# One PSUM tile per bank, 32-bit words in the weight conversion, and a new written order in a fused mLSTM and FFN kernel

## The chip, the core and the metric

The kernel runs on one core of a Trainium2 chip. The metric is the device time of one execution in microseconds (us), as the median of several runs. The engines go by their short names in the profile: PE is TensorE's matmul side and PEld its weight load, DVE is VectorE, ACT is ScalarE, POOL is GpSimd and SP issues the DMAs.

## What is computed

```python
for t in range(S):                    # q,k,v: (4 batches, 8 heads, 768 steps, 40)
    m_new = np.maximum(f_gate[:, :, t] + m, i_gate[:, :, t])
    f_stab, i_stab = np.exp(f_gate[:, :, t] + m - m_new), np.exp(i_gate[:, :, t] - m_new)
    m = m_new
    C = f_stab * C + i_stab * einsum(v_t, k_t);  n = f_stab * n + i_stab * k_t
    y[:, :, t] = sigmoid(o_gate) * (C q_t) / maximum(abs(n . q_t), 1)
x = y as (3072 tokens, 320)
h = x @ w_in                          # (320, 2048)
g = where(h > 0, h, exp(minimum(h, 0)) - 1)
out = g @ w_out                       # (2048, 320)
```

The two weight matrices arrive as 64-bit floats. The matmuls of the FFN take each operand as a high and a low part, and multiply three of the four pairs of parts.

## The kernel before

The tokens are 24 tiles of 128 (n = 0 to 23), six chunks of time for each of four batches. For each tile the attention does, in this order: `kq` and `us` (matmuls into the PSUM tile `pa`), a scan `ws`, products and state updates on DVE or POOL, `y` (matmuls into `pb`), a division, `turn` (three transposes through `pb`), and `xh`, `xl`, the two parts of the FFN's input. Two tiles make a block (kb = 0 to 11), 256 tokens wide.

For each block the FFN runs through 16 slices f of 128 columns of the inner width. One step of it is `L1` (eight matmuls into one bank of the PSUM tile `ph`, banks taken in turns, L659), `relu` (ACT, reads `ph`, L666), `exp` (ACT, in place, L668), `elu` (DVE, reads `ph` again, L670), `gh` (the high part, on ACT, DVE or POOL, L219), `gl` (the low part, on DVE or POOL, L675) and `L2` (six matmuls that add into `pc`, one bank for each of the block's two tiles, L682). There are 12 x 16 = 192 such steps. After a block's last slice, `os` copies `pc` out.

The weights of a group of four slices must be converted first. There are 18 conversions, of 512 or 640 columns: a load of 64-bit words into `wide`, then on the high halves `abs` (L311 or L313), `clip` (L317), `shift` (L321), on the low halves `frac` (ACT, L324), on the high halves `sign` (ACT, L329), then `join` (POOL, L338), `hi` (L345 or L347) and `lo` (DVE, L351). So that matmuls have work while weights are still coming, SPLITS lets some blocks run through part of the width first; the sums of such a part are stored to DRAM and loaded again (`sumstore`, `sumload`).

The first SPREAD_BY_PE tiles get their gate factors by small matmuls (`spread`, `spreadb`, into `ph` or `pc`), all others by DMAs that read them back from DRAM (`wdload`, `bbload`).

PLACES gives each operation its place in one order of the whole program and, by a letter, its engine where there is a choice. Each engine and SP's queue work through their own operations in that order. The semaphores between engines are put in by the framework, from what each instruction reads and writes in which tile. The keys in the calls of `op` only assert that PLACES is a legal order.

Of the kernel before, what the change touches and what calls it, by code (L numbers as in the profile page):

```python
# [19 lines left out]
P = 128  # L20

HI_MIN = 2.0**-14
# [4 lines left out]
    3g 27 6 17 15v 10g 8g 49g 21g 0g 4g 2 26v 35 37 24 30 42 50 58 29 61v 62 63 55 59 68 74 79 36 33 67 75 77 70  # L27
    78 81 85 100 90 104 51 101 109 112 106 110 117 138 144 73 120 147 149 123 127 153 164 168 113 155 173 181 176
    192 210 237 262 154 203 218 230 207 226 240 270 277 175 266 274 279 252 256 284 298 341 219 288 296 308 275
    309 315 326 400 253 350 364 369 321 334 373 383 391 302 404 412 417 397 418 424 451 459 328 325 394v 434 440  # L30
    374 389 444 477 500 507g 512 382 465 471 476 421 435 489 508 516 436 518 523 530 487 520 535 545 552 453 522v
    528 549 492 537 558 575v 590 498 559 564 572 531 565 578 586 595 544 596 605 610 616 624 630 639v 644 566 604
    613 625 642 646 650 659 662 1 9 11 13 12 16 19 14 22 31 53 111 108 18 23a 20 25 7 57v 44 34 52 48 54 56 60 66
    69 65 71 72 76 83 86 89g 91 94 97a 103 115 121 38 41 45 87v 129 64 46 80 93g 82 107 96 116 119 122 125 124 136
    139 140 142 143 145a 146 152 156 5 28 32 39 40 99 47 43 114 135 137 160 162 158 190a 161 170 174 178 180 185
    217 169 184 187 193 196 205 250 182 198 231 238 249 258 261 208 216 236 241 245 260 265 291v 307 272 338 98 95
    92 84 88 131 128 133v 199 126 130 132 151 179 159 172 177 188 194 202 204 206g 209 211 213a 215 220 224 134
    118 141 105 102 157 165 195v 223 163 189g 200 201 225g 212 214 221v 228 232 243 246 247 251 254 257v 259 263
# [12 lines left out]
    708 747 678 684 693 697 699 710 752 705 711 715 723 731 744 767 706 718 721 724 727 748g 773 732 749 750 753
    755 762 776 714 782 786 775 803 831 741 756 760 766 768v 771g 810 761 769 772 778 784g 788g 830 781 789 791
    799 802 807 836 787 794 797 801 818g 824g 862 804 812 814 819 828 835 870 817 847 851 852 853g 854g 890 840
    845 849 866 871g 882g 893 855 864 867 872 891v 894g 898 701 905 952 809 925 1042 569 468 330 509 244 547 335
    675v 734 670 677 636 683 696g 691 682 689 692 698 717 730 738 740g 742 746 751v 757 765 770 614 606 592 293
    619 461 457 720v 737 704 713 712 726 754 785 716v 733 736v 790 798 805v 808 811g 813 816 820a 827 833 837 881
    886 888 892 899 904g 930 884 897 900 903 915v 918g 948 902 910 911 914 916 920g 954 907 921 922 923 927g 949g
    974 924 932 933 939 942v 967 980 935 955 958 962 965 970g 992 960 971 973 977 984 987g 999 968 976 978 983
    986g 989 1003 985 990 991 994 996v 1001 1015 988 995 997 1002 1004g 1007 1020 1000 1005 1006 1009 1010v 1012g
    1024 1008 1013 1014 1016 1018v 1023 1033 1011 1017 1019 1022 1025g 1028g 1047 1027 1030 1031 1034 1038v 1041g  # L60
    1052 1029 1035 1036 1040 1048 1050g 1056 1037 1045 1046 1049 1051 1053 1061 1067v 1106 1073 1324 504 597 501
    603 722 709 780 792v 822 774 779g 793 796 841 826 815 823 838 839 850 856v 857 859 863 869 874a 877 889 895
    743 739 783 777 729 719 745 842v 901 795 800g 843 848 896g 909 832 878 885v 906 919 926 928 929 931 934 940
    944 950 953 439 725 728 758g 860 829 763 936 844 858g 861 951 846 943 947a 1043 1054 1055 1058 1060v 1076g
    1087 1065 1070 1075 1078 1086g 1088g 1109 1069 1080 1082 1092 1096 1115 1130 1094 1100 1104 1108 1114v 1117g
    1135 1099 1118 1120 1122 1136v 1140g 1157 1123 1131 1133 1141 1144 1153 1165 1145 1152 1155 1158 1162v 1163
    1180 1150 1159 1160 1164 1167v 1169g 1183 1161 1166 1168 1171 1172 1176g 1205 1170 1177 1178 1185 1192g 1193
    1215 1174 1181 1182 1191 1204 1208 1227 1194 1201 1203 1210 1214v 1219g 1232 1200 1212 1216 1233 1235g 1237
    1247 1223 1229 1231 1238 1241g 1246g 1251 1236 1243 1245 1248 1249g 1253g 1263 1240 1250 1252 1254 1256 1257
    1268 1274 1316 1288 1534 868 806 821 834 825 865 759 912 981 887 908g 913 917 1032g 957 945 961 964 982 1081  # L70
    1090 1091 1095 1097 1098 1103 1107 1110 1112 1044 880 883 966 873 956 876 1068 1021 998 1063 1077 1079 1105g
    1084 1066v 1083 1085 1101 1119 1125v 1126 1129g 1132 1134 1137a 1142 1147 1149 1255 1260 1262 1264 1266v 1269g
    1298 1258 1265 1267 1270 1271 1273 1317 1272 1277 1278 1280 1284g 1287 1322 1276 1281 1283 1289 1291g 1309
    1330 1293 1300 1310 1320 1323v 1326 1341 1304 1315 1318 1325 1328 1329g 1346 1327 1331 1332 1334 1335 1337
# [100 lines left out]
def tile_mlstm_then_elu_ffn(  # L175
# [29 lines left out]

# [12 lines left out]
    def copy(e, o, i):  # L218
        nc.scalar.copy(o, i) if e == "ACT" else eng[e].tensor_copy(o, i)  # L219
# [568 lines left out]
```

## Time and profile before

| | |
|---|---|
| runs | 573.17 us median of 3 (570.69 to 574.26) |
| the profiled execution | 575.71 us, of which 573.9 us from the first to the last instruction |
| mean granted TensorE clock | 0.985 of full speed |

The profiled execution is 2.5 us above the median and has 1.8 us outside its span. Every row below is from this one execution.

### The profile page before, as it was taken

The numbers are of one execution on the slowest core, as the hardware profiler recorded it, in microseconds if no ns is written. First come the engines' busy times: TensorE is split into PE (matmuls) and PEld (weight loads), VectorE is DVE, ScalarE is ACT, GpSimd is POOL, SyncE is SP. The second block draws the span as 40 slices with busy tenths as digits, with TensorE's granted clock in tenths as the row PEclk, the third lists the DMA queues.
The fourth block names the chain that finished last, engine by engine and source line by source line (L and its number), as shares of the span: only waits on it lengthen the run. The fifth ranks groups of instructions, "written<-read, shape, count | busy, mean of one in ns | idle before, by whom it ended". The sixth has DMA issues, their size and how long they took to land.

```text
span 573.9 us, 15807 instructions
## 1 busy us (share of the span) xinstructions
PE 478.8 (83%) x6574; PEld 441.1 (77%) x6574; DVE 315.8 (55%) x749; ACT 280.0 (49%) x650; POOL 161.7 (28%) x240
## 2 busy tenths in 40 slices
PE   5478887887889888998888889888888989889876
PEld 5467776876889878887777778778878979778765
DVE  6878777666777455654544447455355553334221
ACT  6858988986443344433333334432334434433333
POOL 4313313223244314423133112313211133132111
PEclk9999999899999899999999999998999999989899
DMA  7764454460344401510420322040321400000000
GB/s 218 246 203 161 140 176 132 143 211 17 98 146 115 118 1 30 152 54 28 129 76 2 97 51 64 5 123 2 97 74 44 123 0 3 24 1 1 23 2 23
DMA packets 21951, 48.13 MB, mean 84 GB/s; under 512 B 4184, under 2 KB 10008, under 8 KB 21880
## 3 DMA queue, kind: packets, MB, share of 16 engines
q1 hardware_dynamic: 21880, 47.13, 27.3%
q8 instruction: 51, 0.84, 0.6%
q14 instruction: 20, 0.16, 0.1%
HBM read 41.35 MB, written 5.77 MB: 82 GB/s over the span
## 4 chain that ended last, share of the span: by engine, by line
PE 56%; ACT 20%; DVE 13%; issue 6%; DMA 3%; SPq 1%; POOL 1%; ACTq 0%; POOLq 0%; DVEq 0%
PE ph L659 35%; PE pc L682 14%; DVE e L670 9%; ACT e L666 7%; ACT e L668 6%; PE pb L567 3%; ACT wide L324 2%; DMA f_d<-dec 2%; ACT wide L329 2%; PE pa L507 1%; PE pa L518 1%; ACT gh L219 1%; PE pb L625 1%; DVE w L489 1%; DVE gl L675 1%
## 5 line engine op out<-in xcount | busy, mean ns | idle before, releaser
L659 PE MATMUL ph<-xh,w 128*128 128x256 f32 x960 | 210.1, 300 | 64.4 <-DVE e L670 47.0
L659 PEld LDWEIGHTS ph<-xh,w 128*128 128x128 f32 x960 | 155.6, 194 | 88.8 <-DVE e L670 64.6
L670 DVE SCALAR_TENSOR_TENSOR e<-e,ph 128x256 f32<-128x256 f32 x192 | 80.1, 419 | 200.9 <-ACT e L668 95.9
L666 ACT ACTIVATE e<-ph 128x256 f32<-128x256 f32 x192 | 73.1, 384 | 213.9 <-PE ph L659 163.6
L682 PE MATMUL pc<-w,gh 128*128 128x320 f32 x768 | 176.8, 317 | 0.1
L682 PEld LDWEIGHTS pc<-w,gh 128*128 128x128 f32 x768 | 129.5, 194 | 1.8 <-DVE den L601 0.8
L659 PE MATMUL ph<-xl,w 128*128 128x256 f32 x576 | 126.3, 288 | 0.2 <-issue 0.2
L682 PE MATMUL pc<-w,gl 128*128 128x320 f32 x384 | 121.2, 316 | 1.0 <-DVE gl L675 0.7
L659 PEld LDWEIGHTS ph<-xl,w 128*128 128x128 f32 x576 | 98.0, 194 | 0.2 <-DVE xl L630 0.2
L675 POOL TENSOR_TENSOR gl<-e,gh 128x256 fp32r<-128x256 f32 x76 | 58.6, 772 | 116.8 <-ACT gh L219 55.7
L668 ACT ACTIVATE e<-e 128x256 f32<-128x256 f32 x192 | 79.4, 418 | 5.3
L682 PEld LDWEIGHTS pc<-w,gl 128*128 128x128 f32 x384 | 73.9, 192 | 2.5 <-DVE gl L675 1.6
L219 POOL CAST gh<-e 128x256 fp32r<-128x256 f32 x55 | 25.6, 466 | 136.1 <-DVE e L670 127.8
L675 DVE TENSOR_TENSOR gl<-e,gh 128x256 fp32r<-128x256 f32 x116 | 51.8, 453 | 19.2 <-ACT gh L219 10.7
L219 ACT CAST gh<-e 128x256 fp32r<-128x256 f32 x84 | 33.3, 404 | 30.7 <-DVE e L670 29.4
L338 POOL TENSOR_TENSOR narrow<-narrow,wide 128x512 int32<-128x512 int32 (+1 forms) x18 | 26.0, 1446 | 70.8 <-ACT wide L329 27.8
L489 DVE TENSOR_TENSOR_SCAN w<-w,ones 128x512 f32<-128x512 f32 x22 | 29.6, 1346 | 0.1
L329 ACT ACTIVATE wide<-wide,tiny 128x512 f16<-128x512 f32 (+1 forms) x18 | 28.4, 1578 | 0.3
L324 ACT ACTIVATE wide<-wide 128x512 int16<-128x512 uint32 (+1 forms) x18 | 26.4, 1483 | 2.6 <-DMA wide<-in_w_in 2.6
L567 PE MATMUL pb<-va,w 64*32 64x41 f32 x1536 | 22.0, 207 | 3.4 <-issue 3.3
L567 PE MATMUL pb<-C,qk 40*64 40x41 f32 x704 | 17.5, 233 | 6.1 <-DVE xl L630 3.8
L567 PEld LDWEIGHTS pb<-va,w 64*32 64x32 f32 x1536 | 18.4, 113 | 5.2 <-issue 3.9
(86 smaller groups left out, 420.3 us busy)
## 6 DMA issues: line engine op xcount, KB each, us to landing
vko<-in_vko SPq DMA_DIRECT2D x24, 480.0 KB
qk<-in_qk SPq DMA_DIRECT2D x48, 160.0 KB
w<-f_d SPq DMA_DIRECT2D x44, 128.0 KB
wide<-in_w_out SPq DMA_DIRECT2D x8, 640.0 KB
wide<-in_w_in SPq DMA_DIRECT2D x8, 512.0 KB
out<-os SPq DMA_DIRECT2D x24, 160.0 KB
bb<-b_d SPq DMA_DIRECT2D x44, 80.0 KB
sum<-os SPq DMA_DIRECT2D x10, 160.0 KB
```

Of the source, the lines that this page charges most:

```text
L219: nc.scalar.copy(o, i) if e == "ACT" else eng[e].tensor_copy(o, i)
L324: lambda e: nc.scalar.mul(quarters[:, :, 0], low.bitcast(U32), 2.0**-29),
L329: nc.scalar.activation(quarters[:, :, 1].bitcast(mybir.dt.float16), high.bitcast(F32), AF.Sign, bias=tiny)
L338: lambda e: nc.gpsimd.tensor_add(word, word, low),
L489: lambda e: nc.vector.tensor_tensor_scan(flat, src, ones.rearrange("p h t -> p (h t)"), 0.0, op0=ALU.mult, op1=ALU.add),
L567: nc.tensor.matmul(y[at, two, j, :], a, m, start=(at.start, two) not in begun, stop=False, skip_group_check=True)
L659: nc.tensor.matmul(h, a[g][:, fs], m, start=(i == 0), stop=(i == len(prods) - 1))
L666: lambda e, h=h, ev=ev: nc.scalar.activation(ev, h, AF.Relu, scale=-1.0), (KHP,), (KE,))
L668: lambda e, ev=ev: nc.scalar.activation(ev, ev, AF.Exp, scale=-1.0), (), (KE,))
L670: lambda e, h=h, ev=ev: nc.vector.scalar_tensor_tensor(out=ev, in0=ev, scalar=-1.0, in1=h, op0=ALU.add, op1=ALU.max),
L675: lambda e, gh=gh, gl=gl, ev=ev: eng[e].tensor_sub(gl, ev, gh.bitcast(F32)),
L682: nc.tensor.matmul(pc[:, a, 0:DM], x[:, sl], bw[g][:, j, :], start=(f == f0 and i == 0), stop=(f == f1 - 1 and i == 2))
```

## The change

- `ph` and `pc` were one PSUM tile each, two banks wide. Each becomes a list of two tiles of one bank. `pa` and `pb` stay as they are; their keys are merged to one each.
- In the conversion `frac` and `sign` wrote 16-bit elements, eight bytes apart. Both now write 32-bit words, eight bytes apart, in place over what they read. `shift` (one input) becomes `shiftor`, which also takes the low word as a second input. `join` adds the high word instead of the low one. All 18 conversions take this form (the branch for the other form is never used). `hi` may no longer go to POOL.
- SPLITS has one more entry, (3, 8): four blocks instead of three go through eight of the 16 slices before any goes on.
- SPREAD_BY_PE falls from 2 to 1: tile 1 gets its factors by four DMAs.
- PLACES is new throughout, order and engines (not shown here).

```diff
-    SPLITS = [(0, 4), (1, 4), (0, 8), (1, 8), (2, 8)]
+    SPLITS = [(0, 4), (1, 4), (0, 8), (1, 8), (2, 8), (3, 8)]
+    SIGN_BY_ACT = range(18)
-    SPREAD_BY_PE = 2
+    SPREAD_BY_PE = 1
...
-    ph = psum.tile([P, 2, 512], F32, name="ph")
-    pc = psum.tile([P, 2, 512], F32, name="pc")
+    ph = [psum.tile([P, 512], F32, name=f"ph{x}") for x in range(2)]
+    pc = [psum.tile([P, 512], F32, name=f"pc{x}") for x in range(2)]
...
-           lambda e: nc.vector.tensor_scalar(word, word, 3, None, op0=ALU.logical_shift_left),
...
-           lambda e: nc.scalar.mul(quarters[:, :, 0], low.bitcast(U32), 2.0**-29),
...
-                nc.scalar.activation(
-                    quarters[:, :, 1].bitcast(mybir.dt.float16), high.bitcast(F32), AF.Sign, bias=tiny)
...
+           lambda e: nc.scalar.activation(
+               low, low.bitcast(U32), AF.Copy, scale=2.0**-29, bias=-0.4999 if by_act else 0.0),
...
+            op(f"shiftor {i}", "DVE",
+               lambda e: nc.vector.scalar_tensor_tensor(
+                   out=word, in0=word, scalar=3, in1=low, op0=ALU.logical_shift_left, op1=ALU.bitwise_or),
+               RL, (KN,))
+            op(f"sign {i}", "ACT",
+               lambda e: nc.scalar.activation(high.bitcast(F32), high.bitcast(F32), AF.Sign, bias=tiny),
+               (("tiny", 0),), RH)
...
-           lambda e: nc.gpsimd.tensor_add(word, word, low),
+           lambda e: nc.gpsimd.tensor_add(word, word, high if by_act else low),
...
-            h = ph[:, k % 2, 0:N]
+            h = ph[k % 2][:, 0:N]
...
-                            pc[:, a, 0:DM], x[:, sl], bw[g][:, j, :],
+                            pc[a][:, 0:DM], x[:, sl], bw[g][:, j, :],
```

Counted over the new order: `gh` goes to ACT 84, DVE 66 and POOL 42 times (84, 53 and 55 before), `gl` to DVE 129 and POOL 63 times (116 and 76 before).

## Rows read from the trace of the kernel before

**Rows 1.** Stretches: length, busy PE, PEld, DVE, ACT, POOL, granted clock, DMA share, GB/s.

```profile
0.00:36.00 36.00, 19.43 (x459) 17.17 (x460) 26.48 (x57) 25.43 (x37) 13.30 (x22) 1.00 0.72 215
36.00:203.00 167.00, 140.58 (x2040) 130.13 (x2040) 117.09 (x269) 113.78 (x240) 51.48 (x65) 0.98 0.45 136
203.00:574.00 371.00, 318.80 (x4078) 293.79 (x4078) 172.22 (x424) 140.75 (x373) 96.89 (x155) 0.99 0.16 48
```

**Rows 2.** Who waited for whom, whole span: us in total, times, longest.

```profile
ACT e L666 <- PE ph L659: 163.6, 88, 3.7
...
PEld ph L659 <- DVE e L670: 64.6, 75, 2.0
DVE e L670 <- PE ph L659: 64.2, 40, 4.2
...
PE ph L659 <- DVE e L670: 47.0, 68, 1.7
...
PEld ph L659 <- ACT e L666: 23.1, 28, 1.5
...
PE ph L659 <- ACT e L666: 15.3, 20, 1.4
```

**Rows 3.** Timeline: start, length, instruction [idle time before it, and its releaser].

```profile
299.19 0.45 PE L682 MATMUL pc<-w,gh 128*128 128x320 f32 x2
...
300.07 0.28 PE L659 MATMUL ph<-xh,w 128*128 128x256 f32 x1
...
300.67 0.51 PE L659 MATMUL ph<-xh,w 128*128 128x256 f32 x3
301.29 0.42 DVE L670 SCALAR_TENSOR_TENSOR e<-e,ph 128x256 f32<-128x256 f32 x1 [4.15 <-PE ph L659]
...
301.76 0.39 PE L659 MATMUL ph<-xh,w 128*128 128x256 f32 x1 [0.58 <-DVE e L670]
...
302.47 0.52 PE L659 MATMUL ph<-xh,w 128*128 128x256 f32 x3
...
303.08 0.38 ACT L666 ACTIVATE e<-ph 128x256 f32<-128x256 f32 x1 [2.80 <-PE ph L659]
```

**Rows 4.** Groups by line (the page's section 5): busy, mean ns | idle before.

```profile
L675 POOL TENSOR_TENSOR gl<-e,gh 128x256 fp32r<-128x256 f32 x76 | 58.6, 772 | 116.8 <-ACT gh L219 55.7 <-DVE gh L219 42.9 <-PE pc L682 11.3
L668 ACT ACTIVATE e<-e 128x256 f32<-128x256 f32 x192 | 79.4, 418 | 5.3
...
L675 DVE TENSOR_TENSOR gl<-e,gh 128x256 fp32r<-128x256 f32 x116 | 51.8, 453 | 19.2 <-ACT gh L219 10.7 <-POOL gh L219 6.6 <-PE ph L659 0.5
```

**Rows 5.** Timeline of the attention's matmuls of one tile, PE.

```profile
320.60 0.69 PE L507 MATMUL pa<-qk 40*64 40x64 f32 x32
...
322.14 0.81 PE L567 MATMUL pb<-va,w 64*32 64x41 f32 x64
```

**Rows 6.** Groups by line and shape: the conversion at 512 columns.

```profile
L324 ACT ACTIVATE wide<-wide 128x512 int16<-128x512 uint32 x10 | 13.5, 1351 | 2.6 <-DMA wide<-in_w_in 2.6
...
L329 ACT ACTIVATE wide<-wide,tiny 128x512 f16<-128x512 f32 x10 | 14.4, 1444 | 0.1
...
L311 ACT ACTIVATE narrow<-wide 128x512 f32<-128x512 f32 x6 | 4.0, 666 | 0.0
...
L321 DVE TENSOR_SCALAR narrow<-narrow 128x512 int32<-128x512 int32 x10 | 4.2, 421 | 0.1
...
L351 DVE SCALAR_TENSOR_TENSOR w<-narrow,w 128x512 fp32r<-128x512 f32 x8 | 5.4, 687 | 0.3 <-ACT w L345 0.2
```

**Rows 7.** Timeline, DVE beside POOL, and the mean of that DVE group.

```profile
18.71 1.28 POOL L338 TENSOR_TENSOR narrow<-narrow,wide 128x512 int32<-128x512 int32 x1 [2.35 <-ACT wide L329]
...
19.18 1.16 DVE L459 TENSOR_TENSOR va<-vko,va 128x320 f32<-128x320 f32 x1
...
L459 DVE TENSOR_TENSOR va<-vko,va 128x320 f32<-128x320 f32 x17 | 8.9, 524 | 0.0
```

**Rows 8.** Who waited for whom: the longest wait of an engine for a DMA.

```profile
POOL narrow L338 <- DMA vko<-in_vko: 6.6, 1, 6.6
```

More of the change, by code (lines that the diff above doesn't have):

```diff
@@ new lines @@
+    340 94 102 100 69 71 109 112 137v 205 116 128g 135 144 147 179 150 153v 155 190 202v 204 207g 211 214 217a 218
+    223 226 151 136 142 123 120 172 167 193v 243 187 197g 198 203 208 222 210 213 250 229 236 238 242g 248 254
+    258a 262 266 271 277 287 289 293 297 308 316 281 291 292 298 305 311 324 299 312 315 323 328 330 335 307 319
+    322 327 342 351 359 373 386 370 374 343 347 349 357 376 381 391 345 355 363 365 368 388 395 364 385 393 398
+    409 413 416 369 390 394 401 407 410 423 382 465 477 405 462 467 403 415 419 421 432 436 475 411 427 429 441
@@ new lines @@
+    591 597 612 564 581 585 590 594 601 630 599 609 611 618 623 627 636 642 645 654 658 240 235 313 260 245 265
+    325 417 470 389 399g 379 434 439g 444 371 449 457v 473 455 469 476 478 479 485 487a 490 505 509 377 333 339
+    301 317 285 304 489v 474 424 484g 494 497 528g 532 516v 530 536 548 558 567 569 572g 576 582 589a 595 607 614
+    620 626 629 632 637 657 667 625 631 634 638 644 663 686 641 665 666 670 673 678 691 647 668 671 675 677 682
+    698 674 684 692 696 699 704 718 681 687 690 694 708 712 726 707 715 716 724 731 735 742 713 720 723 728 730v
@@ new lines @@
+    1191 1193 1194 1197g 1238 1188 1196 1199 1201 1204g 1207 1245 1195 1202 1203 1206 1213 1217 1252 1205 1211
+    1212 1215 1218 1223 1265 1209 1221 1222 1225 1243v 1246 1268 1224 1233 1235 1249 1253 1256g 1278 1231 1255
+    1259 1262 1269g 1272 1291 1260 1266 1267 1270 1271v 1274 1296 1273 1276 1277 1279 1281v 1285 1299 1275 1280
+    1282 1284 1287g 1289g 1300 1283 1288 1290 1292 1297g 1303g 1307 1315v 1350 1345v 1559 577 610 613 566 571 729
+    575 759v 897 783 790g 814 817 874 852 795 825 835v 850 878 888v 890 891 900 904 909a 912 1004 1017 676 777 725
@@ new lines @@
+    683 773 661 843 812 936 806 855 859 862 933 870 907 911 927v 928 1071 1079v 1081 1084g 1086 1088 1091 1094
+    1103 1132 1286 1294 1295 1304 1311 1321 1351 1305 1309 1312 1314 1316g 1319g 1358 1313 1325 1326 1329 1335
+    1348g 1367 1317 1322 1328 1332 1352g 1361 1370 1336 1353 1356 1360 1362 1365g 1382 1342 1366 1369 1372 1377v
+    1378g 1387 1363 1368 1373 1374 1376v 1380g 1401 1375 1381 1383 1385 1388 1391 1406 1379 1390 1392 1395 1396v
+    1399 1415 1393 1398 1400 1402 1405g 1411 1426 1397 1403 1404 1407 1408v 1410 1438 1409 1413 1414 1416 1418v
@@ new lines @@
+    1503 1451 1457 1458 1463 1465v 1466 1509 1464 1476 1478 1479 1487 1504g 1514 1468 1472 1475 1494 1497 1501g
+    1517 1490 1510 1513 1515 1516 1518g 1528 1498 1506 1508 1512 1519v 1521g 1550 1520 1524 1530 1539 1542g 1544g
+    1572 1522 1531 1535 1537 1548g 1554 1576 1543 1551 1555 1558 1568v 1570 1579 1557 1564 1565 1573 1580 1582
+    1589 1562 1574 1575 1577 1578 1581 1594 1584 1586 1588 1590 1592v 1595 1604 1585 1591 1593 1596 1597v 1599
+    1610 1598 1602 1603 1605 1611 1616 1622 1601 1606 1608 1614 1617v 1625 1630 1615 1619 1620 1623 1624v 1627
@@ new lines @@
+    1943 1934 1946 2020 1938 2083v 1974 1977 2080 2079 2086 2085g 2144 2102v 2103 2195 2203v 2204 2205 2207 2210
+    2215a 2216 2218 2220 2255 2259 2260 2262 2268v 2271 2279 2257 2263 2264 2266 2267v 2275g 2283 2269 2276 2278
+    2280 2285v 2287 2290 2273 2281 2282 2284 2286 2289 2300 2288 2291 2292 2294 2295g 2298 2304 2293 2297 2299
+    2301 2303 2306 2314 2296 2302 2305 2307 2309 2310g 2322 2308 2312 2313 2315 2318g 2320 2329 2311 2316 2317
+    2321 2323g 2328 2336 2319 2324 2325 2327 2333 2335g 2344 2326 2330 2331 2334 2337v 2339 2354 2332 2338 2340
@@ L129 @@
+    2342 2343g 2352 2357 2341 2345 2346 2348 2349v 2351 2364 2347 2353 2355 2356 2358 2360g 2368 2350 2359 2362
+    2363 2366 2369 2372 2361 2365 2367 2370 2371v 2373 2374 2375 2377 2376 2378
 """
@@ L293, in conversion @@
         low, high = pairs[:, :, 0], pairs[:, :, 1]
-        quarters = both[:, 0 : 2 * n].bitcast(mybir.dt.int16).rearrange("p (n four) -> p n four", four=4)
         word = narrow[i % room["narrow"]][:, 0:n]
+        by_act = i in SIGN_BY_ACT
         KW, KN = ("wide", i % room["wide"]), ("narrow", i % room["narrow"])
-        KL, KS, KH = (KW + (x,) for x in ("low", "sign", "high"))
+        KL, KH = (KW + (x,) for x in ("low", "high"))
         at = 0
@@ L305, in conversion @@
                lambda e, s=s, a=a: nc.sync.dma_start(both[s, 0 : 2 * n].bitcast(I64), a),
-               (), tuple(k + (x,) for k in (KL, KS, KH) for x in parts))
-        RL, RS, RH = (tuple(k + (x,) for x in range(2)) for k in (KL, KS, KH))
+               (), tuple(k + (x,) for k in (KL, KH) for x in parts))
+        RL, RH = (tuple(k + (x,) for x in range(2)) for k in (KL, KH))
         def magnitude(e):
@@ L317, in conversion @@
            lambda e: nc.vector.tensor_scalar(
-               word.bitcast(F32), word.bitcast(F32), HI_MIN, HI_MAX, op0=ALU.max, op1=ALU.min),
-           (), (KN,))
-        op(f"shift {i}", "DVE",
-           lambda e: nc.vector.tensor_scalar(word, word, 3, None, op0=ALU.logical_shift_left),
+               word.bitcast(F32), word.bitcast(F32), LEAST[by_act], HI_MAX, op0=ALU.max, op1=ALU.min),
            (), (KN,))
         op(f"frac {i}", "ACT",
-           lambda e: nc.scalar.mul(quarters[:, :, 0], low.bitcast(U32), 2.0**-29),
-           (), RL + RS)
@@ L327, in unit @@
-        def unit(e):
-            if e == "ACT":
-                nc.scalar.activation(
-                    quarters[:, :, 1].bitcast(mybir.dt.float16), high.bitcast(F32), AF.Sign, bias=tiny)
-            else:
-                nc.vector.tensor_scalar(
-                    quarters[:, :, 1].bitcast(mybir.dt.uint16), quarters[:, :, 3].bitcast(mybir.dt.uint16), 0x8000, 0x3C00,
-                    op0=ALU.bitwise_and, op1=ALU.bitwise_or)
-        op(f"sign {i}", "ACT DVE", unit, RH + (("tiny", 0),), RS)
+           lambda e: nc.scalar.activation(
+               low, low.bitcast(U32), AF.Copy, scale=2.0**-29, bias=-0.4999 if by_act else 0.0),
@@ new lines, in conversion @@
+           (), RL)
+        if by_act:
+            op(f"shiftor {i}", "DVE",
[5 more added lines that the diff above has]
+               (("tiny", 0),), RH)
+        else:
+            op(f"shift {i}", "DVE",
+               lambda e: nc.vector.tensor_scalar(
+                   word, word, 3, 0x3FFFFFFF, op0=ALU.logical_shift_left, op1=ALU.bitwise_and),
+               (), (KN,))
+            op(f"merge {i}", "DVE",
+               lambda e: nc.vector.scalar_tensor_tensor(
+                   out=word, in0=high, scalar=-0x40000000, in1=word, op0=ALU.bitwise_and, op1=ALU.bitwise_or),
+               RH, (KN,))
@@ L337, in conversion @@
         op(f"join {i}", "POOL",
-           lambda e: nc.gpsimd.tensor_add(word, word, low),
-           RL + RS, (KN,))
+           lambda e: nc.gpsimd.tensor_add(word, word, high if by_act else low),
+           RH if by_act else RL, (KN,))
+        up = 2.0 if by_act else 1.0
         for x, (rows, hi, lo) in enumerate(to):
@@ L344, in upper @@
                 if e == "ACT":
-                    nc.scalar.activation(hi[rows], word.bitcast(F32)[rows], AF.Copy, scale=256.0)
+                    nc.scalar.activation(hi[rows], word.bitcast(F32)[rows], AF.Copy, scale=up)
                 else:
-                    eng[e].tensor_scalar(hi[rows], word.bitcast(F32)[rows], 256.0, None, op0=ALU.mult)
+                    eng[e].tensor_scalar(hi[rows], word.bitcast(F32)[rows], up, None, op0=ALU.mult)
             def rest(e, rows=rows, hi=hi, lo=lo):
@@ L351, in rest @@
                 eng[e].scalar_tensor_tensor(
-                    out=to, in0=word.bitcast(F32)[rows], scalar=256.0, in1=hi[rows].bitcast(F32),
+                    out=to, in0=word.bitcast(F32)[rows], scalar=up, in1=hi[rows].bitcast(F32),
                     op0=ALU.mult, op1=ALU.subtract)
-            op(f"hi {i} {x}", "ACT DVE POOL", upper, (KN,), (KO + ("h",),))
+            op(f"hi {i} {x}", "ACT DVE", upper, (KN,), (KO + ("h",),))
             op(f"lo {i} {x}", "DVE", rest, (KN, KO + ("h",)), (KO,))
@@ L469, in attention @@
         if by_pe:
-            fw = spot[:, 0].rearrange("p (h t) -> p h t", t=Q)
-            fb = spot[:, 1, 0 : HH * Q].rearrange("p (j t) -> p j t", t=Q)
+            fw = spot[0].rearrange("p (h t) -> p h t", t=Q)
+            fb = spot[1][:, 0 : HH * Q].rearrange("p (j t) -> p j t", t=Q)
             def spread(e):
@@ L486, in attention @@
             op(f"spreadb {n}", "PE", spread_b, (("gates", g, "c"), ("ident", 0)), (KSP[1],))
-        src = spot[:, 0] if by_pe else flat
+        src = spot[0] if by_pe else flat
         op(f"ws {n}", "DVE",
@@ L557, in attention @@
         else:
-            op(f"gather {n} 0", "ACT DVE", lambda e: copy(e, state(1)[0:R2], us(0)[0:R2]), (KA[0],), (KC[1],))
+            op(f"gather {n} 0", "ACT DVE", lambda e: copy(e, state(1)[0:R2], us(0)[0:R2]), KA, (KC[1],))
         if more:
@@ L697, in ffn @@
                 op(f"os {u} {a}", "DVE",
-                   lambda e, os=os, a=a: nc.vector.tensor_add(os, pc[:, a, 0:DM], os), (KA,), (KOS,))
+                   lambda e, os=os, a=a: nc.vector.tensor_add(os, pc[a][:, 0:DM], os), (KA,), (KOS,))
             else:
-                op(f"os {u} {a}", "ACT DVE", lambda e, os=os, a=a: copy(e, os, pc[:, a, 0:DM]), (KA,), (KOS,))
+                op(f"os {u} {a}", "ACT DVE", lambda e, os=os, a=a: copy(e, os, pc[a][:, 0:DM]), (KA,), (KOS,))
             if f1 < NF:
```

177 lines of the change are left out of this document (70 added, 107 removed), and 5 rows, old and new, of the table PLACES.

## The prediction

> **What bounds the kernel now.** I read the stretches first [rows 1]: in the last 371 us PE is busy 319 us, DVE 172, ACT 141 and POOL 97. So PE is the busiest engine by far, yet it idles 52 us there, and 95 us of the span in all (573.9 less 478.8, the sum of the three). The list of waits says for whom [rows 2]: before `L1` PE sat idle 47.0 us until an `elu` on DVE ended and 15.3 us until a `relu` on ACT ended, 62.3 us together, in 88 waits. That is odd: an `L1` writes a bank of `ph` that the step two before it used, and no `relu` should free a bank, since the `elu` behind it reads the same bank again.
>
> The timeline shows what happens [rows 3]. An `L1` starts at 300.07. Its last three matmuls run from 300.67 to 301.18, and at 301.29 an `elu` starts that had waited for it. This `elu` belongs to the step before, in the other bank, and needs nothing of that `L1`. The next `L1` starts at 301.76, after that `elu`, whose bank it reuses: a true wait. It ends at 302.99, and only then, at 303.08, does a `relu` start. By the written order it is the `relu` of the first `L1`, whose result had been ready since 301.18. So each instruction on `ph` waits for the one before it in program order, whichever bank it is in. I went through the order of all `L1`, `relu` and `elu`: of the 474 neighbours on different engines none overlaps. The sums in [rows 2] agree: `relu` waits 163.6 us for `L1`, `elu` 64.2 us for `L1`. The tile of two banks is followed as one thing, and double buffering doesn't happen.
>
> What a wait costs PE is more than its idle time, because the matmuls in flight drain first. The weight load, which runs ahead, sat idle 64.6 us for `elu` and 23.1 us for `relu` before `L1`, 87.7 us in 103 waits [rows 2]. The drain explains the difference: a matmul lasts 0.28 us and the next follows after 0.12 [rows 3], so 0.16 us of "busy" time per wait is drain, and the first matmul after a wait is longer too (0.39 against 0.28).
>
> **Part 1: `ph` as two tiles.** It removes all order between the banks. What is left for a bank is `L1`, `relu`, `exp`, `elu` and then the `L1` two steps on. From the end of an `L1` that is 0.38 + 0.42 + 0.42 us [rows 3, 4] and some 0.06 us at each of three handovers, 1.4 us. Meanwhile PE has an `L1` (eight matmuls, five of them from 300.07 to 300.67, so 0.96 us) and an `L2` (299.19 to 300.07, 0.88 us) [rows 3]: 1.84 us a step. In the new order all but one of the 190 pairs have at least one `L1` and one `L2` between them, so the chain is covered unless DVE or ACT is busy with something else. From `L1` to its own `L2` the chain goes on over `gh` and `gl` (0.45 us on DVE, 0.77 on POOL [rows 4]), 2.7 us from the end of `L1`; the median work on PE between them is 7.2 us in the new order, and one pair is below 2.7.
> The gain lies between 62.3 us (idle alone) and 87.7 us (with the drains). I take 87.7, since the weight load is what a matmul that needn't wait would follow. What comes back: the scan, the products and the divisions of a tile's attention stand in DVE's queue ahead of some `elu`, where the slack is 0.4 us. I put that at one wait of the size of today's, 0.5 us, for each of 24 tiles: 12 us, between nothing and 30 us (two such waits and a longer one).
>
> **Part 2: `pc` as two tiles.** `os` reads a bank that the next block's `L2` writes, and several steps lie between in the order; before, no wait of PE for `os` is large enough to be listed. Nothing, and at most 12 x 0.5 us if `os` comes late.
>
> **Part 3: the conversion.** `frac` takes 1351 ns and `sign` 1444 ns for 512 elements, where `abs`, which reads the same 8-byte steps but writes 32-bit words side by side, takes 666 [rows 6]. The new forms write 32-bit words 8 bytes apart, which the trace doesn't show. Between 666 and 1444 I take the lower end for `frac` and 0.1 us more for `sign`, as it is the row that differs in the fewest things. That frees 18 x 1.4 = 25 us of ACT. `shiftor` has two inputs like `lo`, 687 ns against 421 for `shift` [rows 6]: 18 x 0.27 = 5 us more of DVE, with one `hi` or `abs` less in places.
> All this falls in the first third. From 36 to 203 us ACT is busy 114 of 167 us and DVE 117 [rows 1], and 57 `L1` begin by 203 us. For the same 57 in the new order I counted operations by kind, at the means of their shapes: ACT 111, DVE 129, PE 124 us. DVE has more because more attention is done early (13 us: `shiftor` 5, three more tiles' pieces 6, `gl` 2). So without the waits on `ph` this stage is bound by DVE, with PE close behind. At 88% busy, which DVE has never had over a long stretch here, 129 us take 147 us: 20 less than now. That is a part of the 87.7 us, not added to it. The relief of ACT is worth perhaps 10 us more, as `relu` no longer stands behind 2.8 us of `frac` and `sign`; bounds 0 and 17 (the 25 us less the third spent before 36 us).
> The Trainium skill, "ScalarE: Activation LUTs", section "What ACT_TABLE_LOAD costs", says that an ACTIVATE takes one element per cycle, for 32-bit and 16-bit data alike. The rows disagree for this form (1351 ns for 512 elements, where `abs` takes 666 [rows 6]); if the width doesn't matter, the 8-byte step of the output must be what costs, and the change keeps that step.
> The same skill, "SBUF — State Buffer", section "SBUF: two separate sides", says that DVE with two SBUF inputs and POOL lock each other out for a whole instruction. A row agrees: a `va` on DVE begins beside a `join` and takes 1.16 us, where its mean is 0.52 [rows 7]. The 18 `shiftor` and 13 more `gl` on DVE are of that kind, but POOL loses 13 `gh` and 13 `gl`, so I leave it out of the sum.
>
> **Part 4: four blocks, one tile spread by PE.** Two more `sumstore`, two `sumload` and two `os` with an addition instead of a copy: about 0.5 us each on DVE beside other work, 1 us if nothing covers them. Tile 1's factors by DMA instead of 48 small matmuls: PE is idle half of the first 36 us [rows 1], and the DMA has to come back before `ws 1`; 3 us either way.
>
> **The sum,** against this execution: 575.7 - 87.7 + 12 - 10 = 490. It lies 2.5 us above the median of the runs, so 488 for the median. A check from the other side: PE's work is 192 x 1.84 = 353 us, 24 tiles at 2.4 us (320.60 to 322.95, [rows 5]) and 7 us of transposes, 418 us. The first `L1` can't come much before 36 us, of which 10 are this work, DVE's stage adds some 20, and the end after the last `L1` I put at 8 us (the step's own chain of some 4 us, two `os` and the store): 472 us with no wait at all later on.
>
> **The rivals.**
> - *The step costs, not the width.* `frac` and `sign` stay at 1351 and 1444 ns. Then ACT has some 17 us more up to the 57th `L1`, 128 us beside DVE's 129, and the 10 us of relief are lost: 498. For it: the step is the same; against it: `abs` reads at that step at full rate.
> - *DVE's queue takes the place of the wait.* The stage with 129 us of DVE work keeps today's 70% (117 of 167), and takes 184 us instead of 147: 488 + 37 = 525. For it: DVE is one queue in a fixed order, and attention and conversion crowd there; against it: much of its idle time today is the very wait on `ph` (64.2 us for `L1`).
> - *The order on `ph` stays,* because the framework puts it in for another reason than the tile. Only ACT's relief is left: 575.7 - 10 - 2.5 = 563. Against it: the serial order is exactly by tile, and `frac` beside `abs` on interleaved halves of one SBUF tile overlap in this trace.
> - *Slower: DVE stands behind a reload.* Each of 12 `os` now adds sums that a `sumload` must bring; that load stands in SP's queue behind loads that wait for a free tile, and every `elu` stands behind the `os`. It needs 88 / 12 = 7.3 us each to lose the whole gain; at 8.5 us the time is 590. The longest wait for a DMA before is 6.6 us, once, on POOL [rows 8], and ten such reloads run now without one on DVE.
>
> **How the numbers follow.** Forecast 488 (470 to 508): 0.57. Step and not width, 498 (485 to 515): 0.14. DVE's queue, 525 (508 to 545): 0.18. Order stays, 563: 0.03. Slower, 590: 0.03. Better than 470: 0.05. From 464 to 526 is 8 in 10: the forecast with the bounds of its returns, the step, and half of the queue's case. A measurement of this kernel can tell about 1% from no change; faster by more than that is 0.95, within it 0.02, slower 0.03.
>
> **What would show it.** Right: in the list of waits, `relu` for `L1` falls from 163.6 us to below 60 and the weight load's idle time before `L1` from 87.7 to below 30; a `relu` starts 0.1 us after its own `L1`, while the next `L1` runs; `frac` and `sign` at 512 columns take 0.65 to 0.8 us. Wrong: idle time before `L1` as before but ended by `elu` alone (the queue), DVE's busy share in the first 200 us at 70% or below, or waits of `os` for a load.

## The result and the profile after

The changed kernel takes 478.2 us (median of 4 runs, 477.8 to 483.2) where the kernel before, beside it, took 573.3: a ratio of 0.837, 95% interval 0.831 to 0.843. The forecast was 488 with a range of 464 to 526. The profiled execution took 477.8 us, 97.9 less than the 575.7 of the profile before; the sum had said 490 for it.

The head of the page of the changed kernel, and its chain of work that ended last, by engine and by line:

```profile
span 476.0 us, 15778 instructions
PE 444.6 (93%) x6526; PEld 428.7 (90%) x6526; DVE 331.3 (70%) x781; ACT 258.4 (54%) x655; POOL 143.3 (30%) x205
...
PE 72%; DVE 9%; DMA 8%; ACT 6%; issue 4%; POOL 1%; SPq 0%; DVEq 0%; POOLq 0%; ACTq 0%
PE ph L665 32%; PE pc L688 30%; PE pb L573 4%; DMA sum<-os 2%; PE pa L513 2%; DMA wide<-in_w_out 2%; PE pa L524 2%; DVE gl L681 2%; DVE e L676 2%; ACT e L674 1%; DMA bb<-b_d 1%; ACT e L672 1%; PE pb L631 1%; DVE w L495 1%; DMA qk<-in_qk 1%
```

PE is idle 31 us of the span now, after 95, and its busy time has fallen too, from 478.8 to 444.6 us. The stretches of the changed kernel, with the columns of [rows 1], show where that lies:

```profile
0.00:36.00 36.00, 19.68 (x424) 17.41 (x424) 29.64 (x62) 19.60 (x42) 13.57 (x23) 1.00 0.79 222
36.00:203.00 167.00, 157.54 (x2569) 149.63 (x2569) 144.03 (x319) 115.22 (x283) 59.16 (x71) 0.98 0.54 158
203.00:476.00 273.00, 267.40 (x3537) 261.69 (x3535) 157.59 (x402) 123.62 (x330) 70.61 (x113) 1.00 0.18 54
...
36.00:180.00 144.00, 134.77 (x2257) 127.18 (x2257) 126.97 (x278) 105.61 (x258) 51.49 (x58) 0.98 0.59 172
...
62.00:70.00 8.00, 8.00 (x233) 7.58 (x231) 7.74 (x17) 6.56 (x17) 2.44 (x3) 1.00 0.77 240
70.00:78.00 8.00, 7.43 (x79) 6.66 (x79) 7.90 (x13) 5.69 (x17) 3.78 (x5) 1.00 0.50 153
```

From 203 us on PE idles 5.6 us, where it idled 52 [rows 1]. Of the idle time that is left, 16 us lie in the first 36. The 57th `L1` starts at 178.9 us (before 202.8), the last one at 468.3 (before 564.5): of the 97.9 us, 23.9 were won before the 57th, 72.3 from there to the last, 1.7 behind it.

The waits of the changed kernel (who for whom, us in total, times, longest), to be laid beside [rows 2] and [rows 8]:

```profile
DVE e L676 <- ACT e L674: 92.9, 98, 3.2
ACT e L672 <- PE ph L665: 89.3, 61, 5.4
...
POOL C L551 <- DMA bb<-b_d: 28.4, 1, 28.4
...
ACT e L672 <- DVE gl L681: 20.6, 23, 2.4
...
ACT e L672 <- POOL gl L681: 15.5, 11, 2.3
...
PEld ph L665 <- DVE e L676: 4.5, 11, 1.0
POOL vko L499 <- DMA sum<-os: 4.1, 1, 4.1
```

The weight load's 87.7 us of idle time ahead of `L1` have become 4.5, and of its idle time for `relu` no line is listed. DVE still waits for the exponential of its own step (92.9 us, before 95.9), but no longer for an `L1` of the next one (before 64.2). The long wait for a DMA, 28.4 us, is POOL's, once. The timeline of the changed kernel shows the new order on `ph` (start, length, instruction, idle time before it and its releaser; PE's weight loads and the rest of DVE left out):

```profile
301.19 0.28 PE L665 MATMUL ph<-xh,w 128*128 128x256 f32 x1
...
301.78 0.64 PE L665 MATMUL ph<-xh,w 128*128 128x256 f32 x4
...
302.35 0.39 ACT L672 ACTIVATE e<-ph 128x256 f32<-128x256 f32 x1 [1.60 <-PE ph L665]
302.39 0.28 PE L665 MATMUL ph<-xh,w 128*128 128x256 f32 x1
302.50 0.41 PE L665 MATMUL ph<-xl,w 128*128 128x256 f32 x2
302.75 0.52 PE L665 MATMUL ph<-xh,w 128*128 128x256 f32 x3
...
303.21 0.42 DVE L676 SCALAR_TENSOR_TENSOR e<-e,ph 128x256 f32<-128x256 f32 x1 [1.06 <-ACT e L674]
...
303.99 0.28 PE L665 MATMUL ph<-xh,w 128*128 128x256 f32 x1
...
304.46 0.38 ACT L672 ACTIVATE e<-ph 128x256 f32<-128x256 f32 x1 [0.91 <-DVE gl L681]
304.58 0.52 PE L665 MATMUL ph<-xh,w 128*128 128x256 f32 x3
```

Two `L1` run back to back from 301.19, eight matmuls each (the row of four from 301.78 holds the last three of the first and the first of the second). The first one's `relu` starts at 302.35, while the second fills the other bank up to 303.27. In [rows 3] the `relu` could only start behind the next `L1`. Over the whole trace, 453 neighbours on `ph` are on different engines and 187 of them overlap (before none of 474); the median `relu` starts 0.10 us behind its own `L1` (before 1.06). The `relu` at 304.46 shows the next limit: it waited for `gl`, which frees the buffer `e`.

Conversion of the changed kernel by line and shape (busy, mean ns, idle before), beside [rows 6]:

```profile
L322 ACT ACTIVATE wide<-wide 128x512 int32<-128x512 uint32 x10 | 6.8, 678 | 1.2 <-DMA wide<-in_w_in 1.2
L331 ACT ACTIVATE wide<-wide,tiny 128x512 f32<-128x512 f32 x10 | 7.7, 770 | 0.2
L327 DVE SCALAR_TENSOR_TENSOR narrow<-narrow,wide 128x512 int32<-128x512 int32 x10 | 6.9, 686 | 0.4
L357 DVE SCALAR_TENSOR_TENSOR w<-narrow,w 128x512 fp32r<-128x512 f32 x8 | 5.9, 742 | 0.0
...
L681 DVE TENSOR_TENSOR gl<-e,gh 128x256 fp32r<-128x256 f32 x129 | 59.5, 470 | 13.2 <-POOL gh L220 5.6 <-ACT gh L220 3.9 <-PE ph L665 0.5
L681 POOL TENSOR_TENSOR gl<-e,gh 128x256 fp32r<-128x256 f32 x63 | 47.2, 754 | 80.6 <-DVE gh L220 25.6 <-PE pc L688 23.7 <-ACT gh L220 18.5
```

`frac` fell from 1351 to 678 ns and `sign` from 1444 to 770, with the output's step of eight bytes kept. `shiftor` costs the 0.27 us over `shift` that were put in.

### The profile page after: what moved, and what is told of

The parts are those of the page before. It is cut to its first block, busy times and chain, and to the rows that moved or that the text cites. A ratio compares the mean times of both kernels' runs of the same rounds, so it can differ in the third digit from the quotient of the medians.

```text
span 476.0 us, 15778 instructions
## 1 busy us (share of the span) xinstructions
PE 444.6 (93%) x6526; PEld 428.7 (90%) x6526; DVE 331.3 (70%) x781; ACT 258.4 (54%) x655; POOL 143.3 (30%) x205
## 4 chain that ended last, share of the span: by engine, by line
PE 72%; DVE 9%; DMA 8%; ACT 6%; issue 4%; POOL 1%; SPq 0%; DVEq 0%; POOLq 0%; ACTq 0%
PE ph L665 32%; PE pc L688 30%; PE pb L573 4%; DMA sum<-os 2%; PE pa L513 2%; DMA wide<-in_w_out 2%; PE pa L524 2%; DVE gl L681 2%; DVE e L676 2%; ACT e L674 1%; DMA bb<-b_d 1%; ACT e L672 1%; PE pb L631 1%; DVE w L495 1%; DMA qk<-in_qk 1%
## 5 line engine op out<-in xcount | busy, mean ns | idle before, releaser
L665 PE MATMUL ph<-xh,w 128*128 128x256 f32 x960 | 194.5, 289 | 2.4 <-DVE e L676 1.8
L688 PE MATMUL pc<-w,gh 128*128 128x320 f32 x768 | 174.2, 314 | 0.2 <-ACT gh L220 0.2
L665 PEld LDWEIGHTS ph<-xh,w 128*128 128x128 f32 x960 | 152.1, 192 | 5.5 <-DVE e L676 4.5
L672 ACT ACTIVATE e<-ph 128x256 f32<-128x256 f32 x192 | 72.8, 381 | 139.5 <-PE ph L665 89.3
L676 DVE SCALAR_TENSOR_TENSOR e<-e,ph 128x256 f32<-128x256 f32 x192 | 79.1, 417 | 94.1 <-ACT e L674 92.9
L688 PEld LDWEIGHTS pc<-w,gh 128*128 128x128 f32 x768 | 125.8, 189 | 1.3 <-ACT gh L220 0.3
L688 PE MATMUL pc<-w,gl 128*128 128x320 f32 x384 | 119.5, 311 | 0.2 <-DVE gl L681 0.2
L681 POOL TENSOR_TENSOR gl<-e,gh 128x256 fp32r<-128x256 f32 x63 | 47.2, 754 | 80.6 <-DVE gh L220 25.6
L681 DVE TENSOR_TENSOR gl<-e,gh 128x256 fp32r<-128x256 f32 x129 | 59.5, 470 | 13.2 <-POOL gh L220 5.6
L220 POOL CAST gh<-e 128x256 fp32r<-128x256 f32 x42 | 19.6, 467 | 95.3 <-DVE e L676 71.3
L220 DVE CAST gh<-e 128x256 fp32r<-128x256 f32 x66 | 20.4, 314 | 5.8 <-PE pc L688 2.2
L573 PEld LDWEIGHTS pb<-C,qk 40*64 40x64 f32 x704 | 14.4, 138 | 7.2 <-issue 4.0
```

The lines of the kernel that those rows point to most:

```text
L573: nc.tensor.matmul(y[at, two, j, :], a, m, start=(at.start, two) not in begun, stop=False, skip_group_check=True)
L665: nc.tensor.matmul(h, a[g][:, fs], m, start=(i == 0), stop=(i == len(prods) - 1))
L672: lambda e, h=h, ev=ev: nc.scalar.activation(ev, h, AF.Relu, scale=-1.0), (KHP,), (KE,))
L676: lambda e, h=h, ev=ev: nc.vector.scalar_tensor_tensor(out=ev, in0=ev, scalar=-1.0, in1=h, op0=ALU.add, op1=ALU.max),
L681: lambda e, gh=gh, gl=gl, ev=ev: eng[e].tensor_sub(gl, ev, gh.bitcast(F32)),
L688: nc.tensor.matmul(pc[a][:, 0:DM], x[:, sl], bw[g][:, j, :], start=(f == f0 and i == 0), stop=(f == f1 - 1 and i == 2))
```

## The experiments

The theory was the prediction's: the split of `ph` brings nearly all, the conversion some 10 us, `pc` and the new order nothing. The rival was that the order, written out anew with four early blocks, brings a good part, and that the split alone leaves DVE's queue in its place. Times are medians; ratios are to the kernel before, run beside it (571.9 to 573.3 us).

**The split alone** (old_split): the kernel before with one tile per bank, its own order and conversion.

```diff
-    ph = psum.tile([P, 2, 512], F32, name="ph")
-    pc = psum.tile([P, 2, 512], F32, name="pc")
+    ph = [psum.tile([P, 512], F32, name=f"ph{x}") for x in range(2)]
+    pc = [psum.tile([P, 512], F32, name=f"pc{x}") for x in range(2)]
...
-            h = ph[:, k % 2, 0:N]
+            h = ph[k % 2][:, 0:N]
```

> The kernel before, with ph and pc as two tiles of one bank each and nothing else: old order, old conversion, two tiles spread by PE. Theory 1 (the order between the two banks of ph is what cost the time): most of the 87.7 us that the weight load waited before L1 goes, 485 to 505 us, and the waits of relu for L1 fall from 163.6 us to below 80. Theory 2 (the new written order brings the gain, and the tiles only permit it): 530 to 560 us, because the old order leaves L1 standing behind elu anyway.

Measured: 485.3 us, ratio 0.848 [0.843, 0.852]. The split takes 87.8 us from the old order. A few of them may be the granted clock: its means were 0.993 to 1.000 in these runs and 0.979 to 0.993 in those of the kernel before beside them; at 0.993, which both have, 487.4 stands against 569.2 and 572.9, 82 to 86 us. Its waits:

```profile
ACT e L666 <- PE ph L659: 79.2, 70, 3.6
...
PEld ph L659 <- DVE e L670: 9.2, 12, 1.7
...
PE ph L659 <- DVE e L670: 6.4, 7, 1.5
```

**The split undone** (new_one_ph): the changed kernel with `ph` as one tile again.

```diff
-    ph = [psum.tile([P, 512], F32, name=f"ph{x}") for x in range(2)]
+    ph = psum.tile([P, 2, 512], F32, name="ph")
...
-            h = ph[k % 2][:, 0:N]
+            h = ph[:, k % 2, 0:N]
```

> The changed kernel with ph alone put back into one tile of two banks; pc stays split, and order and conversion are the new ones. Theory 1: the waits come back, about as many as before, 555 to 580 us, and no relu starts before the following L1 has ended. Theory 2: the new order holds most of the gain, 490 to 520 us.

Measured: 557.1 us, ratio 0.973 [0.968, 0.978], 78.9 us above the changed kernel. The rows of [rows 2] come back nearly whole, and of the 453 neighbours on `ph` again none overlaps:

```profile
ACT e L672 <- PE ph L665: 169.4, 84, 5.9
...
PEld ph L665 <- DVE e L676: 62.3, 78, 1.6
DVE e L676 <- PE ph L665: 60.7, 36, 5.4
...
PEld ph L665 <- ACT e L672: 19.3, 24, 1.5
```

The weight load's idle time for `elu` and `relu` is 81.6 us here and 4.5 in the changed kernel: 77.1 of the 78.9 us.

**The order alone** (new_one_conv16): the changed kernel with both tiles joined again (the diff above, and the same for `pc`) and the old conversion, so that the order, the four early blocks and the single spread are left.

```diff
-    ph = [psum.tile([P, 512], F32, name=f"ph{x}") for x in range(2)]
-    pc = [psum.tile([P, 512], F32, name=f"pc{x}") for x in range(2)]
+    ph = psum.tile([P, 2, 512], F32, name="ph")
+    pc = psum.tile([P, 2, 512], F32, name="pc")
...
-               low, low.bitcast(U32), AF.Copy, scale=2.0**-29, bias=-0.4999 if by_act else 0.0),
+           lambda e: nc.scalar.mul(quarters[:, :, 0], low.bitcast(U32), 2.0**-29),
```

> The new order alone: the changed kernel with ph and pc as tiles of two banks and with the old conversion. If the order is worth something only together with split tiles: 568 to 578 us. If the three parts add: the new order with ph in one tile (557) plus the 6 to 12 us of the conversion, 563 to 569.

Measured: 571.4 us, ratio 0.999 [0.995, 1.002]. By itself the order is worth nothing. The sum of parts fails here: between new_one_ph and this kernel lie 14 us, where 6 to 12 were expected for the conversion.

**Everything but the order** (old_split_conv32): the kernel before with the split of old_split and the new conversion in the old order (`sign` moved behind `abs` in five conversions, `shiftor` behind `frac` in two, one `hi` from POOL to DVE).

```diff
+    ph = [psum.tile([P, 512], F32, name=f"ph{x}") for x in range(2)]
...
+               low, low.bitcast(U32), AF.Copy, scale=2.0**-29, bias=-0.4999 if by_act else 0.0),
...
+               lambda e: nc.scalar.activation(high.bitcast(F32), high.bitcast(F32), AF.Sign, bias=tiny),
```

> The kernel before with both PSUM tiles split and the new conversion, in the old order. If the three parts add, the old order with split tiles (485) loses another 6 to 12 us: 473 to 480, level with the changed kernel, and the new order with its fourth early block is worth nothing by itself. If the new order matters once the tiles are split, it stays above 482.

Measured: 477.9 us, ratio 0.837 [0.832, 0.841], the changed kernel's time without its order. The rival falls: from 573.0 the split leads to 485.3, the conversion to 477.9, and the order to 478.2.

**The conversion alone, and undone** (old_conv32, new_conv16): the same conversion in the kernel before without the split, and the old one in the changed kernel (`frac` and `sign` change places in three conversions).

```diff
-               lambda e: nc.scalar.activation(high.bitcast(F32), high.bitcast(F32), AF.Sign, bias=tiny),
+                nc.scalar.activation(
+                    quarters[:, :, 1].bitcast(mybir.dt.float16), high.bitcast(F32), AF.Sign, bias=tiny)
```

> The kernel before with the new conversion alone (32-bit words; the same order, except that sign moves behind abs in five conversions and shiftor behind frac in two, and one hi moves from POOL to DVE). Theory 1: the order on ph still sets the pace, so freeing ACT gives 0 to 10 us, 563 to 573. Rival (ACT bounds the first third of the kernel before): 25 us freed on ACT come back as 15 us or more, 558 or less.

> The changed kernel with the old conversion: frac and sign write 16-bit elements and shift has one input; in three conversions frac and sign change places, as sign must come after frac there. Prediction's term: ACT gets 25 us more work in the first third, and the time rises by 10 us (0 to 17) to 478 to 496. Rival: beside a DVE that is busy 88% of the stage from 36 to 180 us, ACT has room for all of it, and the time stays within 3 us of 478.

Measured: old_conv32 566.7 us, ratio 0.989 [0.985, 0.993]; new_conv16 489.7, ratio 0.856 [0.851, 0.860]. So the conversion is worth 6 us ahead of the split, 7 behind it in the old order and 11.5 in the new one. A stretch of new_conv16:

```profile
36.00:180.00 144.00, 128.25 (x2176) 118.32 (x2175) 115.98 (x262) 117.66 (x248) 45.63 (x52) 0.98 0.55 164
```

ACT is busy 117.7 us in this stretch, where the changed kernel has 105.6, and has become as full as DVE; PE does 81 matmuls fewer. Whether that is why the conversion is worth more here is not shown: in the old order ACT goes from 110.7 us (old_split) to 97.6 (old_split_conv32) in the same stretch, 13 us too, and the time falls by 7.

With this, eight kernels hold every choice of the three parts, leaving `pc` aside (medians, us):

| | neither | conversion | split | both |
|---|---|---|---|---|
| old order | 573.0 | 566.7 | 485.3 | 477.9 |
| new order | 571.4 | 557.1 | 489.7 | 478.2 |

The split is worth 79 to 89 us by what stands beside it, the conversion 6 to 14. The order is worth nothing with neither and with both, but some 10 us beside the conversion alone, and it costs up to 4.4 beside the split alone (1.5 to 3 at the granted clock of 0.993 that both have). So the parts don't simply add.

**`pc` as one tile** (new_one_pc).

```diff
-    pc = [psum.tile([P, 512], F32, name=f"pc{x}") for x in range(2)]
+    pc = psum.tile([P, 2, 512], F32, name="pc")
```

> The changed kernel with pc alone put back into one tile of two banks. Prediction's step (pc as two tiles is worth nothing): within 2 us of 478. Rival: a block's first L2 now also waits for the second os of the block before, 12 times up to 0.5 us, 480 to 484.

Measured: 478.2 us, ratio 0.835 [0.831, 0.840]: nothing.

**What bounds now: DVE early or late** (new_dve_early, new_dve_late): one more addition on DVE, of constants and read by nobody, ahead of `elu` in 56 steps; the first 56, or steps 120 to 175.

```diff
+    LOADED = (0, 56)
...
+                if LOADED[0] <= k < LOADED[1]:
+                    flat = ones.rearrange("p h t -> p (h t)")
+                    nc.vector.tensor_add(spare, flat[:, 0 : TMAX * L], flat[:, TMAX * L : 2 * TMAX * L])
```

> The changed kernel with one more DVE addition of 256 columns (about 0.45 us, on data that nobody uses) ahead of elu in each of the first 56 steps, 25 us of DVE work. Theory A (the prediction's: DVE bounds the stage from 36 to 180 us, where it is 88% busy): 10 to 25 us longer, 488 to 503. Theory B (PE bounds that stage too, and DVE has slack): under 5 us longer.

> The same 25 us of DVE work, in steps 120 to 175, where DVE is about 59% busy. Both theories: PE covers it, 478 to 482.

Measured: 493.1 us early and 481.1 late, against 478.2. The added group in the early run, and its stretch:

```profile
L680 DVE TENSOR_TENSOR spare<-ones 128x256 f32<-128x256 f32 x56 | 34.9, 623 | 0.0
...
36.00:180.00 144.00, 125.30 (x2101) 113.63 (x2102) 139.54 (x305) 99.09 (x240) 44.28 (x48) 1.00 0.55 163
```

and in the late run:

```profile
L680 DVE TENSOR_TENSOR spare<-ones 128x256 f32<-128x256 f32 x56 | 25.1, 448 | 0.0
```

Early, 34.9 us on DVE cost 15, and the 57th `L1` came 13.5 us later (192.4); late, 25.1 us cost 3, inside the spread of the runs. DVE sets the pace only in the first stage, and there not alone: it could still fill up from 127 to 140 us of 144.

**What bounds now: PE** (new_pe_less): without the product `gh` x `w2l`, which is left out of the computation: 384 matmuls, some 56 us of PE.

```diff
-                    for i, (x, bw) in enumerate(((gh, w2l), (gh, w2h), (gl, w2h))):
+                    for i, (x, bw) in enumerate(((gh, w2h), (gl, w2h))):
```

> The changed kernel without one of the three products of L2 (high part of the activations times low part of the weights), so 384 matmuls of 0.147 us, 56 us of PE work, are left out of the computation. If PE bounds it throughout: 56 us less, 420 to 426. If DVE bounds the stage up to 180 us: only the part of it after that, 37 to 45 us, 433 to 441. If the chain of a step takes over everywhere: over 450.

Measured: 455.7 us, ratio 0.795 [0.791, 0.799]: 22.5 us less. That is neither of the two outcomes in which PE sets the pace throughout or behind 180 us, but the third, over 450. The waits of the profiled execution, the slowest of its four (459.1 us):

```profile
ACT e L672 <- DVE gl L681: 32.3, 32, 2.7
...
PEld ph L665 <- DVE e L676: 25.8, 46, 2.3
...
ACT e L672 <- POOL gl L681: 21.0, 18, 2.7
...
PE ph L665 <- DVE e L676: 14.4, 25, 2.1
```

With a shorter `L2` PE waits for `elu` again (the weight load 25.8 us, after 4.5), and this time it is a true wait, on the same bank. `relu`, which stands ahead of that `elu`, waits 53 us for the `gl` that frees its buffer `e` (36 in the changed kernel). The changed kernel's PE stands only a little ahead of the chain of a step.

**Relieving DVE** (new_gl_pool): 23 of the 47 `gl` that DVE does early go to POOL, by their letters in the order.

```diff
-    180 184 209 173 183 185 196 201 220 234 181 195 200 228 237 241 246 221 227 232 257 261 263 270 295 321 303v
+    220g 234 181 195 200 228 237 241 246 221 227 232 257 261 263g 270 295 321 303v 340 94 102 100 69 71 109 112 137v
```

> The changed kernel with 23 of the 47 gl that DVE does in the first 56 steps moved to POOL, at the same places in the order: 11 us less on DVE, 17 us more on POOL. If DVE's load sets the pace there, by what the added load cost (15 us for 35 us of DVE time): 3 to 5 us faster, 473 to 475. If what counts is that gl comes earlier or that POOL locks DVE out: no gain or a loss, 478 to 484.

Measured: 482.8 us, ratio 0.844 [0.841, 0.847]: 4.6 us slower, not faster. Its `gl` on POOL and its stretch:

```profile
L678 POOL TENSOR_TENSOR gl<-e,gh 128x256 fp32r<-128x256 f32 x86 | 71.7, 838 | 101.0 <-ACT gh L217 35.6 <-DVE gh L217 33.6 <-PE pc L685 12.7
...
36.00:180.00 144.00, 133.93 (x2233) 125.43 (x2233) 123.21 (x253) 105.96 (x258) 71.66 (x77) 0.98 0.58 171
```

DVE's busy time in the stretch fell by 3.8 us only (126.97 to 123.21). Over the whole span DVE does the same operations less the 23 `gl`, 11 us by their means (129 of 470 ns before, 106 of 466 now), and its busy time falls by 3.0 us (331.3 to 328.3). A `gl` on POOL rose from 754 to 838 ns. So most of what DVE gave up came back as longer operations. The loss lies in this stage: the 57th `L1` starts at 182.9 us, 4.0 later than in the changed kernel.

## Why the prediction was right

**The split.** Right, as to place and size. Term 87.7, measured 87.8 by itself and 78.9 with the other parts in place; the bound of 62.3 from PE's own idle time was too low. That the two numbers agree to 0.1 us is luck: the weight load's idle time ahead of `L1` fell by 78.5 us in old_split (87.7 to 9.2), and the rest came from elsewhere. The reason given for the difference to 62.3 (the drain) fits: PE's busy time fell from 478.8 to 444.2 us for the same 6574 matmuls, though part of that is the granted clock, 0.985 and 1.000 in these two executions. Against fixed lengths for each kind of PE work (0.96 us an `L1`, 0.88 an `L2`, from [rows 3]) the time lost ahead of `L1` fell from 94.7 to 16.4 us in old_split, and ahead of `L2` from 20.8 to 11.0, which the sum didn't have.

**The 12 us that come back.** This is the term that was mis-sized. The weight load idles 9.2 us for `elu` in old_split and 4.5 in the changed kernel. The 9.2 are made up by what `L2` won, and the changed kernel's sum without this term, 575.7 - 87.7 - 10 = 478.0, is its measured 477.8. That this sum comes so close is luck as well: with the conversion and the order put in first they bring 16 us (573.0 to 557.1) and the split 79. The attention's work does stand ahead of `elu` in DVE's queue; that `L2` hides it is argued from the order, not measured. An `L2` lies between an `L1` and the second one after it in 176 of 190 pairs of the old order and in 180 of the new one. The prediction's count, all but one with an `L1` and an `L2`, holds only if the attention's matmuls are let stand for the `L2` in nine pairs.

**The conversion.** Right: 678 and 770 ns lie inside the 0.65 to 0.8 us named. The 10 us measured as 6 to 14 (557.1 for new_one_ph against 571.4 for new_one_conv16 is the 14). What sets the size is open; how full ACT is doesn't sort them, since from 36 to 180 us it is busy 110.7 us in old_split (worth 7) and 112.6 in new_one_conv16 (worth 14). The rival *step, not width* falls with those two rows. The Trainium skill, "ScalarE: Activation LUTs", section "What ACT_TABLE_LOAD costs", gives one element a cycle for fp32 and bf16 alike. The rows disagree for writes of 16 bits (int16 and f16) eight bytes apart, which took twice the time of 32-bit words at the same step.

**The stage bound by DVE.** 126.97 of 144 us are 88%, as put, and the 57th `L1` starts at 178.9 where 183 was worked out. The early and late loads show that DVE counts there and not later, but by less than one for one (15 for 35). The rival *DVE's queue* (70% kept, 525) falls.

**Parts 2 and 4.** Nothing, as put: 478.2 with `pc` joined, 0.999 for the order alone and 478.2 against 477.9 with the other parts in place. The four blocks and the single spread were not run apart from the order. The slower rival, a reload that holds DVE, doesn't show. The chain that ended last does run over the stores and reloads of `sum` once, from 61.6 to 76.1 us, but DVE is busy 15.6 of the 16 us from 62 to 78 and PE 15.4; the longest wait listed for `sum` is POOL's, 4.1 us, once.

**What would show it.** One sign was wrong: `relu` still waits 89.3 us for `L1`, not under 60. That wait is now ACT being early for its own `L1`, which is no loss; the bar was set on an engine with idle time to spare. The weight load's idle time (under 30; 4.5) was the sign to go by.

**The check from the other side,** 472 us without later waits, lies 4 below the span of 476.0. Its terms don't fit one by one: it has 20 us for DVE's stage, where PE idles 9.5 us from 36 to 203 us, and 418 us of work on PE, which is busy 444.6. That it comes so close is luck.

## What to carry to other kernels

Before double buffering is believed, look in the timeline for a consumer of one half that starts while the other half is being filled; where neighbours never overlap, give each half a tile of its own. Price a wait of PE by the idle time of its weight load, not by that of its matmuls. When one wait goes, ask how much work of the bounding engine stands behind the next one: here it was enough, and taking 56 us from PE then brought only 22.5.

## What was not expected of the hardware

A two-input addition on DVE took 623 ns on average in the first stage and 448 later, for the same shape. The trace of new_dve_early shows what made the difference, since these additions read nothing but constants (start, length, instruction; the rows of DVE and POOL alone):

```profile
123.15 1.59 POOL L345 TENSOR_TENSOR narrow<-narrow,wide 128x640 int32<-128x640 int32 x1 [5.64 <-ACT e L674]
...
123.17 0.42 DVE L681 SCALAR_TENSOR_TENSOR e<-e,ph 128x256 f32<-128x256 f32 x1
123.50 1.52 DVE L680 TENSOR_TENSOR spare<-ones 128x256 f32<-128x256 f32 x1
...
142.32 0.42 DVE L680 TENSOR_TENSOR spare<-ones 128x256 f32<-128x256 f32 x1
```

The addition at 123.50 begins beside a `join` on POOL and ends 0.28 us after it; the one at 142.32 has no instruction on POOL beside it. Of the 56 early additions 26 had none and took 410 ns on average, 420 at most; all 15 that took over 600 ns (630 to 1799) had begun behind a two-input instruction on POOL. Of the 56 late ones 34 had none, and they took 416 ns. So it is not the stage but what POOL does beside them. The `elu` at 123.17, whose second input lies in PSUM, took its 0.42 us beside the same `join`. The Trainium skill, "SBUF — State Buffer", section "SBUF: two separate sides", says that instructions of DVE with two SBUF inputs and those of POOL that read SBUF lock each other out for a whole instruction. These rows agree with it. In the same stage `lo`, an unchanged two-input instruction, rose from 687 to 742 ns.

In new_gl_pool the granted clock from 36 to 110 us was 0.95, where the changed kernel had 0.98, but from 36 to 180 us it was 0.98 in both, and over the whole executions 0.992 and 0.993. The two profiled executions differ by 3.9 us, so the clock explains little of the loss; whether the longer operations on DVE or the later `gl` from POOL make it stays open. That the conversion of 18 chunks is worth 6 to 14 us by the surroundings, and that the split and the conversion together leave the order nothing to do, was measured; why, and why the new order does not use its four early blocks for more, is open too.
